# Where a planner may emit products of zeros, and where ScalarE's queue carries the first loads

## The chip, the cores and the metric

The kernel runs on one NeuronCore of a Trainium2 chip. The metric is the device time of one execution in microseconds (us); the median of three runs before is 318.51 us (318.28 to 318.63). The profile speaks of five engines: PE (matrix products; PEld is its weight load), DVE (vector), ACT (scalar), POOL (general) and SP (which here only issues transfers).

## The reference

A gated linear attention feeds a mixture of four attention experts. Cut to what is computed:

```python
# stage 1: q, k, v, alpha are (4, 8, 768, 48); state starts at 0
for t in range(S):
    state = alpha[:, :, t, :, None] * state + k[:, :, t] outer v[:, :, t]
    y[:, :, t] = q[:, :, t] @ state
x = y, heads side by side            # (4, 768, 384)
# stage 2: for each of 4 experts e, heads of 64
q, k, v = x @ wq[e], x @ wk[e], x @ wv[e]
a = softmax(causal(q @ k.T / 8))
ye = a @ v @ wo[e]
out += (e in the top 2 of x @ w_gate) * softmax_of_top2 * ye
```

## The kernel before

Stage 1 is cut into 24 chunks of 128 steps (6 for each of 4 batches); per chunk `n` the decays `alpha` become running products (two scans on DVE, `prep_r` and `prep_c`), are multiplied into queries and keys (`prep_kq`), and PE forms the chunk's inner products (`gla_a`, line 217), turns the keys (`gla_t`, line 234), updates the state (`gla_u`, line 263) and forms the output (`gla_y`, line 302). Three chunks make a unit; there are 8. Per unit stage 2 projects (lines 325 and 351), scores (400), takes exponentials on ACT (425), scales by the gate on POOL (437), turns the probabilities (452), multiplies with values (477) and with the output weights (496), and stores.

The order of all this is written by a planner in `run` (line 767). It holds, for each engine, the time at which it thinks the engine free (`free`), takes the candidate with the best value, emits it, and goes on. All engines run their emitted list in order and wait on semaphores. Eight PSUM banks `g0` to `g7` (matmul outputs) are handed out by the same planner.

Two places matter here. First, where the planner expects PE to sit idle for more than `IDLE` = 0.1929 us before the next operation, it fills the gap (lines 842 to 847): it takes the bank that comes free first, and `warm(i, k)` (line 884) emits products of a tile `d1r` with itself into that bank, `64 * k` columns wide, at most 512 a call. Nothing reads the result (the tile holds small constants; the title calls these products of zeros). Each call is one 32-bit product that PE runs as two passes, so the profile has two records a call. Line 847 then marks the bank as taken up to the planned start, with or without the products. Second, `opening` (line 892) writes the start by hand: SP issues the two halves of chunk 0's decays (`load_al(0, i, SY)`), ACT copies a one-element tile, ACT issues the two halves of chunk 0's queries and keys (`load_q(0, i, A)`), the constants are set up (mostly on POOL, among them the identity `ident`, line 157), and ACT copies the negated identity into `nid` (line 915), which waits for POOL. Then SP issues the loads of the next chunks and of the weights, and `warm(7, 32)` (line 939) emits four calls of 512 columns.

Transfers signal their landing on eight semaphores, DMAHW0 to DMAHW7, that are given out in turn; the ninth transfer takes the first one's semaphore again, and its issuer first waits until that earlier transfer has landed.

Of the kernel before, what the change touches and what calls it, by code (L numbers as in the profile page):

```python
# [12 lines left out]
AF = mybir.ActivationFunctionType  # L13
# [13 lines left out]
P = 112  # L27
# [9 lines left out]
    P="t.0 u.0 a.0 wx.v.0 a.1 t.1 wx.v.1 y.0 u.1",  # L37
    V="r.0.0 c.0.0 r.0.1 c.0.1 kq.0.0 kq.0.1 r.1.0 c.1.0 kq.1.0 r.2.0 m.1.1 m.1.0 S.1 c.2.0 kq.2.0 xl.0 sa.1 kt.2 xl.1 kr.2 m.2.1 m.2.0 r.3.0 c.3.0",
    A="kr.0 kt.0 wvh m.0.1 m.0.0 wl.v.0 kt.1 kr.1 B.1 wl.v.1 wqh.0 xh.0 xh.1 B.2 vo.0.0 wqh.1 xh.2 kt.3 vo.0.1 ph.0.0.0 ph.0.0.1 woh ck.0 vo.0.2 ck.2 kr.3 B.3",
# [8 lines left out]
CHANGE.update({(x, "y"): 0.12 for x in "tfas"})  # L48
CHANGE.update({(x, "t"): 0.15 for x in "asy"})
CHANGE.update({(x, "f"): 0.2 for x in "asy"})  # L50
IDLE = 0.1929
SHARE = 0
HEAD = 0.012
# [10 lines left out]
def tile_gla_moe(ctx: ExitStack, tc: tile.TileContext, qk_d, al_d, v_d, wqk_d, wv_d, wo_d, nat_d, vn_d, out_d):  # L64
    nc = tc.nc
    V, A, G, PE, SY = nc.vector, nc.scalar, nc.gpsimd, nc.tensor, nc.sync
# [62 lines left out]
    ident = fixed("ident", [128, 128])  # L129
# [17 lines left out]
    nid = fixed("nid", [128, 128], F32R)  # L147

    def constants():
        G.memset(d1r, TINY)  # L150
        G.memset(d1r[:, :, 0:1], 1.0)
        for t in d1c:
            V.memset(t, TINY)
        G.memset(mask, 1.0)
        G.affine_select(mask, mask, [[1, C]], OP.is_ge, 0.0, base=-(C - 1), channel_multiplier=1)
        G.memset(ident, 0.0)
        G.affine_select(ident, ident, [[1, 128]], OP.not_equal, 1.0, base=0, channel_multiplier=-1)
        for t in ST:
            G.memset(t, 0.0)
        for t in unit["kt"]:  # L160
            G.memset(t.rearrange("t p (s d) -> t p s d", s=2)[:, :, :, D:64], 0.0)
        G.memset(acc, 0.0)
        for t in SM:
            G.memset(t, 0.0)
        for t in [t for i, t in enumerate(unit["T"]) if i not in WHOLE]:
            for r in (32, 96):
                G.memset(t[r:r + 32, 3], 0.0)
        G.memset(cmask, 0.0)
        G.affine_select(cmask[:, 384:512], cmask[:, 384:512], [[-1, 128]], OP.is_ge, -1.0e30, base=0, channel_multiplier=1)
        G.memset(lm, 0.0)  # L170
        G.affine_select(lm, lm, [[1, NE], [-1, NE]], OP.is_gt, SMALL, base=0, channel_multiplier=0)
# [588 lines left out]
    for u in range(NU):  # L760
        k = len(ops)
# [5 lines left out]
    def run(start, arrive, busy):  # L767
        ENG = "PVAGS"
        free = dict.fromkeys(ENG, start)
# [35 lines left out]
        while todo:  # L805
            best = {}
            for o in cand:
                base = None
                need = {}
                for name in o["take"]:  # L810
                    pool = POOL.get(name[0], name[0])
                    need[pool] = need.get(pool, 0) + 1
                room = []
                for pool, k in need.items():
                    z = sorted((s[0], s[1]) for s in slots[pool] if s)
                    if len(z) < k:
                        room = None
                        break
                    room.append(z[k - 1])
                if room is None:  # L820
                    continue
                for alt in o["alts"]:
                    e = alt[0]
                    if first[e] and first[e][0] != o["key"] or e not in bound.get(o["key"], e):
                        continue
                    t = free[e]
                    for d in o["deps"]:
                        x, f = done[d]
                        t = max(t, x + hand(f, e) + (MARGIN if e == "P" else 0.0))
                    for x, f in room:  # L830
                        t = max(t, x + hand(f, e))
                    if e == "P":
                        t = max(t, free[e] + SWITCH * CHANGE.get((mode, o["mode"]), 0.0))
                    if e == "G" or o["lock"] and e == "V":
                        t = max([t] + [x[1] for x in lock["V" if e == "G" else "G"][-4:] if x[0] <= t])
                    v = t - free[e] + (PULL[e] if free[e] > 34.0 or e == "S" else HEAD) * (o["target"] - free[e])
                    if e not in best or v < best[e][0]:
                        best[e] = (v, t, o, alt)
            assert best, [o["key"] for o in cand][:30]
            e = min(best, key=lambda x: best[x][1])  # L840
            _, t, o, alt = best[e]
            if e == "P" and free["P"] > start and t - free["P"] > IDLE:
                x, i = min((s[0], i) for i, s in enumerate(slots["g"]) if s)
                k = int((t - max(x, free["P"]) - IDLE) / 0.11)
                if k > 0:
                    warm(i, k)
                    slots["g"][i] = [t, "P"]
            for name in o["take"]:
                pool = POOL.get(name[0], name[0])
                i = min((s[0], i) for i, s in enumerate(slots[pool]) if s)[1]  # L850
                slots[pool][i] = None
                where[name] = (pool, i)
            cand.remove(o)
            if first[e]:
                first[e].pop(0)
            alt[2]()
            dur = alt[1] * (SLOW if e in "VAG" else 1.0)
            end = t + dur
            free[e] = max(end - LAP[e], t + 0.04)
            if o["lock"] == 1 and e == "V":  # L860
                lock["V"].append((t, end))
            if e == "G":
                lock["G"].append((t, end))
            if e == "P":
                mode = o["mode"] or mode
            if o["land"]:
                busy = max(busy, t + 1.2) + KB.get(o["key"][0], 0.0) / RATE
                end = max(end + o["land"], busy)
            for name in o["uses"]:
                give(name, end, e)  # L870
            if len(alt) > 3:
                k = dict(key=o["key"], target=o["target"], deps=[("half", o["key"])], alts=[alt[3]], uses=[], take=[], mode="", land=0.0,
                         lock=False, n=0)
                done["half", o["key"]] = (end, e)
                cand.append(k)
                continue
            done[o["key"]] = (end, e)
            todo -= 1
            for w in waiting.get(o["key"], ()):
                w["n"] -= 1  # L880
                if not w["n"]:
                    cand.append(w)

    def warm(i, k):
        while k > 0:
            n = 64 * min(k, 8)
            PE.matmul(unit["g"][i][:, 0:n], zb[:, 0:128], zb[:, 0:n], start=True, stop=True)  # L887
            k -= 8
# [3 lines left out]
    def opening():  # L892
        arrive, z = {}, [LEAD]

        def came(key, kb):
            z[0] += kb / RATE
            arrive[key] = (z[0], "S")

        for n in range(4):
            where["T", n] = ("T", n)  # L900
        for n in range(3):
            where["v", n] = ("v", n)
        where["al", 0] = ("at", 0)
        plain = list(range(UNITS["al"]))
        for n in range(1, 4):
            where["al", n] = ("a", (2 * n - 2, 2 * n - 1)) if n in WHOLE else ("al", plain.pop(0))
        where["at", "wqk"], where["at", "wvo"] = ("at", 1), ("at", 2)
        for i in (0, 1):
            load_al(0, i, SY)
        G.memset(ones, 1.0)  # L910
        A.activation(ones, ones, AF.Copy)
        for i in (0, 1):
            load_q(0, i, A)
        constants()
        A.activation(nid, ident, AF.Copy, scale=-1.0)
        for key, kb in (("La", 0, 0), 264), (("La", 0, 1), 264), (("Lq", 0, 0), 262), (("Lq", 0, 1), 262):
            came(key, kb)
        z[0] += 0.3
        for n in (1, 2):
            load_al(n, 0, SY)  # L920
            load_q(n, 0, SY)
            load_v(n - 1)
            came(("La", n, 0), 132 * tiles(n))
            came(("Lq", n, 0), 131 * tiles(n))
            came(("Lv", n - 1), 262)
            if n == 1:
                SY.dma_start(wv, wv_d)
                came(("Lw", 1), 400)
        SY.dma_start(wqk, wqk_d)
        came(("Lw", 0), 786)  # L930
        load_v(2)
        came(("Lv", 2), 262)
        load_al(3, 0, SY)
        load_q(3, 0, SY)
        came(("La", 3, 0), 396)
        came(("Lq", 3, 0), 393)
        SY.dma_start(wo, wo_d)
        came(("Lw", 2), 393)
        warm(7, 32)
        return arrive, z[0]  # L940
# [159 lines left out]
```

## Time and profile before

| | |
|---|---|
| median of three runs | 318.51 us |
| the profiled execution | 318.76 us, of it 317.0 us from the first to the last instruction |
| granted TensorE clock, mean | 0.996 |
| line 887 (the products of line 887 in all) | 54 records, 27 calls |
| POOL busy | 128.2 us (40%) |
| ACT busy | 208.9 us (66%) |

Busy time is an average over the whole span; an engine that is busy all the time need not be doing work that the result needs. The chain of waits is the list of what ended last, followed back from the end: what stands on it sets the time, so long as nothing else is close behind. A window row gives the busy time of each engine in a stretch; the number in front of the engines is the stretch's length.

### The profile page before, as it was taken

The page shows a single profiled execution, that of the slowest core. Times are in us where ns is not written, and L with a number is a line of the kernel's source. Part 1 is how long each engine was busy: PE and PEld are TensorE (multiplying, and loading weights), DVE is VectorE, ACT ScalarE, POOL GpSimd, SP SyncE. Part 2 cuts the span into 40 slices and gives each one's busy share as a digit, 9 for nine tenths or more (in the row PEclk, how much of TensorE's full clock was granted, in tenths as well). Part 3 has the DMA queues.
Part 4 walks back from the last instruction along what each step waited for, and adds up shares of the span by engine and source line. Part 5 has one row for each costly group of instructions (what it writes and reads, how often), then busy time and mean ns, then how long its engine had stood idle before and what let it go on. Part 6 is the DMA issues. An engine that isn't in the chain of part 4 may idle for free.

```text
span 317.0 us, 11044 instructions
## 1 busy us (share of the span) xinstructions
PE 308.2 (97%) x4410; PEld 265.4 (84%) x4410; DVE 249.5 (79%) x678; ACT 208.9 (66%) x588; POOL 128.2 (40%) x197
## 2 busy tenths in 40 slices
PE   8999999999999999999999999999999999999992
PEld 3699989898997979889997988889897988888692
DVE  5999899998999998898998989675865754487620
ACT  2464986796785868578775776655964765377841
POOL 6334137516463483526343226414280344033510
PEclk9999999999999999999999999999999999999998
DMA  7996275543526246524354334304100000102001
GB/s 246 389 377 192 70 233 184 156 125 93 158 71 193 84 108 179 146 66 119 106 170 94 117 84 153 90 8 136 41 2 2 3 2 25 53 0 77 2 30 60
DMA packets 26893, 35.21 MB, mean 111 GB/s; under 512 B 2288, under 2 KB 22864, under 8 KB 26832
## 3 DMA queue, kind: packets, MB, share of 16 engines
q1 hardware_dynamic: 26144, 33.69, 34.6%
q8 instruction: 37, 0.61, 0.8%
q10 hardware_dynamic: 688, 0.72, 0.7%
q14 instruction: 24, 0.20, 0.2%
HBM read 27.61 MB, written 4.72 MB: 102 GB/s over the span
## 4 chain that ended last, share of the span: by engine, by line
PE 95%; DMA 1%; DVE 1%; ACT 0%; issue 0%; ACTq 0%; DVEq 0%
PE g L325 16%; PE g L452 13%; PE g L477 12%; PE g L302 11%; PE g L400 11%; PE g L351 8%; PE g L496 8%; PE g L217 7%; PE g L887 3%; PE g L263 2%; PE g L234 2%; DMA at<-in_al_dram 1%; DVE at L178 1%; PE g L721 0%; DVE T L198 0%
## 5 line engine op out<-in xcount | busy, mean ns | idle before, releaser
L437 POOL TENSOR_SCALAR a<-a,cf,gw 128x128 f32<-128x128 f32 (+5 forms) x96 | 80.5, 851 | 71.4 <-DVE cf L431 45.5
L425 ACT ACTIVATE a<-a,mx 128x256 f32<-128x256 f32 (+3 forms) x96 | 51.5, 539 | 9.1 <-DVE mx L414 9.0
L452 PE MATMUL g<-ident,a 128*128 128x128 f32 x336 | 53.7, 277 | 0.0
L325 PE MATMUL g<-x,wqkh 128*128 128x384 f32 x192 | 51.7, 350 | 0.0
L229 POOL TENSOR_SCALAR_AFFINE_SELECT ms<-ms 128x512 f32<-128x512 f32 x31 | 22.1, 724 | 56.2 <-ACT ms L225 56.2
L452 PEld LDWEIGHTS g<-ident,a 128*128 128x128 f32 x336 | 39.7, 140 | 5.8 <-issue 2.3
L240 DVE COPY at<-g 128x512 f32<-128x512 f32 (+3 forms) x62 | 29.2, 479 | 16.9 <-PE g L452 15.9
L477 PE MATMUL g<-at,vg 128*32 128x384 f32 (+2 forms) x648 | 39.7, 389 | 0.0
L400 PE MATMUL g<-k,q 64*128 64x256 f32 (+3 forms) x384 | 39.2, 336 | 0.0
L238 ACT ACTIVATE at<-g 128x512 f32<-128x512 f32 (+3 forms) x66 | 30.4, 465 | 8.4 <-PE g L452 6.6
L477 PEld LDWEIGHTS g<-at,vg 128*32 128x32 f32 x648 | 19.3, 109 | 18.5 <-issue 15.3
L302 PE MATMUL g<-ms,v 128*32 128x128 f32 x768 | 33.0, 274 | 0.0
L325 PEld LDWEIGHTS g<-x,wqkh 128*128 128x128 f32 x192 | 33.0, 189 | 0.0
L400 PEld LDWEIGHTS g<-k,q 64*128 64x128 f32 x384 | 28.6, 185 | 5.2 <-issue 2.3
L325 PE MATMUL g<-x,wqkl 128*128 128x384 f32 x96 | 32.3, 337 | 0.0
L351 PE MATMUL g<-wvh,x 128*128 128x260 f32 x144 | 31.7, 296 | 0.0
L414 DVE CUSTOM_DVE_ANT_0 a<-g,cmask 128x128 f32<-128x128 f32 (+2 forms) x64 | 28.2, 483 | 2.0 <-PE g L400 1.8
L496 PE MATMUL g<-woh,yy 128*128 128x384 f32 x96 | 28.1, 351 | 0.0
L217 PE MATMUL g<-T 48*128 48x128 f32 x384 | 25.7, 275 | 0.0
L217 PEld LDWEIGHTS g<-T 48*128 48x128 f32 x384 | 24.0, 187 | 1.3 <-DVE T L198 0.4
L351 PEld LDWEIGHTS g<-wvh,x 128*128 128x128 f32 x144 | 24.0, 190 | 0.4 <-ACT ms L225 0.4
L302 PE MATMUL g<-T,S 112*32 112x128 f32 x480 | 24.2, 272 | 0.0
(113 smaller groups left out, 616.1 us busy)
## 6 DMA issues: line engine op xcount, KB each, us to landing
al<-in_al_dram SPq DMA_DIRECT2D x21, 387.0 KB, 3.9
T<-in_qk_dram SPq DMA_DIRECT2D x21, 384.0 KB, 4.2
v<-in_v_dram SPq DMA_DIRECT2D x24, 256.0 KB, 4.5
out_dram<-ot SPq DMA_DIRECT2D x23, 192.0 KB, 2.1
T<-T SPq DMA_DIRECT2D x42, 48.2 KB, 2.2
a<-in_al_dram SPq DMA_DIRECT2D x2, 516.0 KB, 6.7
T<-in_qk_dram SPq DMA_DIRECT2D x2, 512.0 KB, 7.1
at<-in_wqk_dram SPq DMA_DIRECT2D x1, 768.0 KB, 8.5
```

The lines of the kernel that those rows point to most:

```text
L217: PE.matmul(pa[s][:, C * p:C * p + C], t[r:r + D, p, C:2 * C], t[r:r + D, p, 0:C], start=True, stop=True, tile_position=(r, 0))
L238: A.activation(out, src, AF.Copy)
L240: V.tensor_copy(out, src)
L302: PE.matmul(o[32 * j:32 * j + 32, k], l, r, start=(i == 0), stop=(i == len(parts) - 1), tile_position=(0, 32 * j))
L325: PE.matmul(pj[:, :W3], w[:, kt, cs], x[:, kt, :], start=(i == 0), stop=(i == 8))
L351: PE.matmul(pv[:, 0:260], x[:, kt, 128 * i:128 * i + 128], w[:, kt, :], start=(m == 0), stop=(m == 8))
L400: PE.matmul(sc(u, pair, i, e, x, c1 - c0), q[r, i0, ts], k[r, i1, c0:c1], start=(y == 0), stop=(y == 2), tile_position=(64 * e, 0))
L425: A.activation(a[:, c0:c1], src, AF.Exp, bias=mx[:, 1:2], scale=-1.0 if last else 1.0, accum_out=sm[:, x:x + 1])
L437: G.tensor_scalar(a[:, 0:n], a[:, 0:n], CF[u % 2][:, 3 * pair + i, e:e + 1], gw[:, u, i, eg:eg + 1], op0=OP.mult, op1=OP.mult)
L452: PE.transpose(pt[:, 128 * (j - j0):128 * (j - j0) + 128], a[:, 128 * j:128 * j + 128], ident)
L477: PE.matmul(o[r:r + 32, lo:n1], v[:, j % 3, 64 * eg + x:64 * eg + x + 32], at(("at", u, pair, e))[:, min(j, 4), at_off(j) + lo:at_off(j) + ...
L496: PE.matmul(po[:, 0:DM], y[:, h, 128 * i:128 * i + 128], w[:, pair, :], start=(m == 0), stop=(m == 5))
```

## The change

A constant `START` = 32.0 is added; the gap filler emits its products only where the planner's time for PE is below it. The mark on the bank is kept, so every later choice of the planner stays as it was. In the opening, the constants and the copy into `nid` are written before the two loads of chunk 0's queries and keys on ACT.

```diff
+START = 32.0
@@ run
                 k = int((t - max(x, free["P"]) - IDLE) / 0.11)
                 if k > 0:
-                    warm(i, k)
+                    if free["P"] < START:
+                        warm(i, k)
                     slots["g"][i] = [t, "P"]
@@ opening
         A.activation(ones, ones, AF.Copy)
+        constants()
+        A.activation(nid, ident, AF.Copy, scale=-1.0)
         for i in (0, 1):
             load_q(0, i, A)
-        constants()
-        A.activation(nid, ident, AF.Copy, scale=-1.0)
```

Of the 27 calls 16 go: their widths are 64, 192, 64 and 448 columns in PE's list up to its 45th us, then six of 64, and near the end 320, 128, 64, 128, 64 and 128. PE's list is otherwise the same, operation for operation and bank for bank. The fourth of them stands between two outputs of stage 1 (`ms`, `v`, `T`, `S` are masked products, values, queries with keys, and state). PE before:

```order
202 L302 MATMUL g_104<-ms_67,v_92 32x128 x8
203 L302 MATMUL g_104<-T_85,S_114 32x128 x4
204 L887 MATMUL g_105<-d1r 128x448
205 L302 MATMUL g_106<-ms_68,v_93 32x128 x4
206 L302 MATMUL g_106<-T_86,S_115 32x128 x4
```

And now, PE at the same place:

```order
199 L303 MATMUL g_104<-ms_67,v_92 32x128 x8
200 L303 MATMUL g_104<-T_85,S_114 32x128 x4
201 L303 MATMUL g_106<-ms_68,v_93 32x128 x4
202 L303 MATMUL g_106<-T_86,S_115 32x128 x4
203 L303 MATMUL g_106<-ms_68,v_93 32x128 x4
```

One call is gone and its neighbours have closed up; the second output still goes to the same bank.

The other place is the head of ACT's list, with the semaphores that each row waits for (`T_85` holds chunk 0's queries and keys). ACT before:

```order
2 L911 ACTIVATE ones<-ones 128x1 [waits Pool_49]
3 L122 DMA T_85<-in_qk_dram 128x2x256 x2
4 L915 ACTIVATE nid<-ident 128x128 [waits Pool_49]
5 L238 ACTIVATE kt_69<-g_101 128x3x2x16 [waits PE_49]
6 L238 ACTIVATE kt_69<-g_101 128x6x48
```

And now, ACT:

```order
2 L913 ACTIVATE ones<-ones 128x1 [waits Pool_49]
3 L915 ACTIVATE nid<-ident 128x128 [waits Pool_49]
4 L123 DMA T_85<-in_qk_dram 128x2x256 [waits DMAHW0_49]
5 L123 DMA T_85<-in_qk_dram 128x2x256 [waits DMAHW1_49]
6 L239 ACTIVATE kt_69<-g_101 128x3x2x16 [waits PE_49]
```

The two loads have moved behind the copy, and each has got a wait: they are now the ninth and tenth transfer in the order in which the semaphores are given out, and so wait for the landing of the first and the second, which are the two halves of chunk 0's decays on SP. In turn two SP loads, of chunk 2's decays and of its queries and keys, have lost theirs. SP before (`a` and `at_63` hold decays, `at_65` and `at_64` weights, `v` values):

```order
5 L927 DMA at_65<-in_wvg_dram 128x780
6 L118 DMA a<-in_al_dram 128x2x516 [waits DMAHW0_49]
7 L122 DMA T_87<-in_qk_dram 128x4x256 [waits DMAHW1_49]
8 L125 DMA v_93<-in_v_dram 128x512 [waits DMAHW2_49]
9 L929 DMA at_64<-in_wqk_dram 128x1536 [waits DMAHW3_49]
```

And now, SP:

```order
5 L929 DMA at_65<-in_wvg_dram 128x780
6 L119 DMA a<-in_al_dram 128x2x516
7 L123 DMA T_87<-in_qk_dram 128x4x256
8 L126 DMA v_93<-in_v_dram 128x512 [waits DMAHW2_49]
9 L931 DMA at_64<-in_wqk_dram 128x1536 [waits DMAHW3_49]
```

SP's order is the same; only what its sixth and seventh rows wait for has changed.

## Rows read from the trace of the kernel before

**Rows 1.** The page: busy time of two engines, and the chain by engine and line.

```profile
PE 308.2 (97%) x4410; PEld 265.4 (84%) x4410; DVE 249.5 (79%) x678; ACT 208.9 (66%) x588; POOL 128.2 (40%) x197
...
PE 95%; DMA 1%; DVE 1%; ACT 0%; issue 0%; ACTq 0%; DVEq 0%
```

**Rows 2.** PE's waits, whole span: total, times, longest (us).

```profile
PE g L234 <- issue: 0.6, 1, 0.6
PE g L234 <- ACT ms L225: 0.4, 1, 0.4
```

**Rows 3.** The chain of waits, 30 to 46 us: start, length, what.

```profile
32.27 0.36 PE g L887 x2
...
38.92 0.52 PE g L887 x2
...
41.76 0.36 PE g L887 x2
...
44.93 0.95 PE g L887 x2
```

**Rows 4.** Timeline of PE, 41 to 43 us: start, length, engine, line, tiles.

```profile
41.69 0.43 PE L887 MATMUL g<-d1r 128*128 128x64 f32 x2
41.93 0.37 PE L351 MATMUL g<-wvh,x 128*128 128x260 f32 x1
```

**Rows 5.** Windows: two stretches, then busy time of each engine in them.

```profile
32.00:64.00 32.00, 31.59 (x527) 27.95 (x514) 29.22 (x80) 25.48 (x74) 14.52 (x24) 1.00 0.53 159
76.00:290.00 214.00, 214.00 (x3001) 187.97 (x3003) 171.50 (x487) 145.76 (x419) 86.54 (x120) 1.00 0.29 84
```

**Rows 6.** DVE's waits, 30 to 64 us.

```profile
DVE cf L430 <- ACT a L425: 0.9, 2, 0.7
...
DVE kt L240 <- PE g L234: 0.4, 1, 0.4
DVE st L272 <- PE g L263: 0.3, 1, 0.3
```

**Rows 7.** The chain of waits, 145 to 148 us.

```profile
146.31 0.36 PE g L887 x2
```

**Rows 8.** The chain of waits, 288 to 311 us.

```profile
293.18 0.74 PE g L887 x2
...
300.38 0.22 PE g L887 x2
...
308.16 0.36 PE g L887 x2
```

**Rows 9.** Timeline, ACT and PE, 293 to 294 us.

```profile
293.01 0.86 ACT L238 ACTIVATE at<-g 128x512 f32<-128x512 f32 x2
...
293.76 0.83 PE L452 MATMUL g<-ident,a 128*128 128x128 f32 x6
```

**Rows 10.** Transfers issued up to 4 us: KB each, median us to landing.

```profile
at<-in_al_dram SPq DMA_DIRECT2D x2, 258.0 KB, 4.2
...
T<-in_qk_dram ACTq DMA_DIRECT2D x2, 256.0 KB, 3.4
...
v<-in_v_dram SPq DMA_DIRECT2D x1, 256.0 KB, 6.5
```

**Rows 11.** The chain of waits, 0 to 9.5 us.

```profile
0.81 3.84 DMA at<-in_al_dram
...
7.84 1.28 DVE T L198 x2
```

**Rows 12.** Timeline of PE from 10.4 us, and of SP up to 4 us.

```profile
3.52 0.66 SPq L125 DMA_DIRECT2D v<-in_v_dram  x1
...
10.50 0.29 PE L263 MATMUL g<-v,kt 128*32 128x48 f32 x8
```

**Rows 13.** Groups of PE by form, up to 6.8 us, then 9.2 to 10.25.

```profile
L887 PE MATMUL g<-d1r 128*128 128x512 f32 x6 | 5.5, 1088 | 1.6 <-POOL d1r L151 1.6
...
L887 PE MATMUL g<-d1r 128*128 128x512 f32 x2 | 1.0, 594 | 0.0
```

## The prediction

> **What bounds the kernel now.** I read the busy times and the chain first, then PE's waits, then the pieces of the chain that are products of zeros, then windows. PE is busy 97% of the span and holds 95% of the chain [rows 1]. After the opening it waits twice, 0.6 us before its first key transposes and 0.4 us for one mask copy on ACT [rows 2]. So PE's list, played back to back, sets the time, and the reader is to see that products of zeros stand in that list as on the chain: 0.36, 0.52, 0.36 and 0.95 us for the first four that go [rows 3], 0.36 us for each of the six of 64 columns in the middle [rows 7], and 0.74, three of about 0.2 (one shown, 0.22) and 0.36 us near the end [rows 8]. A sixteenth comes after the last output product, when only ACT's copy and the store are left, and counts nothing. The planner put them where it expected PE to idle; the trace shows no idle time around them. What the rows can't say by themselves is whether PE would have waited there without them, so each stretch needs its own look at the engines behind PE.
>
> **First part: the zeros that go.** Gross, by the chain, they are 2.19 + 6 x 0.36 + 1.7 = 6.05 us. I take that apart in three.
>
> *30 to 64 us, 2.19 us gross.* Here PE is not alone. From 32 to 64 us PE is busy 31.59 of 32 us, and VectorE 29.22 [rows 5]: it has 2.78 us to spare, and part of that it spends waiting for ACT. If PE comes earlier, VectorE can follow only by waiting less for PE. Of its waits in this stretch 0.4 + 0.3 = 0.7 us are for PE, and the longest is 0.9 us for ACT [rows 6]. So of 2.19 us I expect PE to keep about 0.6; the rest comes back as waits of PE, on VectorE's or ACT's results, by the wait on ACT at the end of the stretch at the latest. The bounds are 0 (VectorE and ACT set the pace here alone) and 2.19 (all kept).
>
> *64 to 290 us, six calls.* VectorE is busy 171.50 and ACT 145.76 of 214 us, PE all 214 [rows 5], and PE has no wait of note in that stretch [rows 2]. What is cut from PE here is kept. How much one call is worth has two readings: 0.36 us in the chain, or 0.24 us from its first start to the next product's start, 41.69 to 41.93 [rows 4], which I use for this form since all calls of 64 columns look alike. The next product's first pass is itself longer behind a call of zeros, and without the call some of that stays, since a change from narrow to full weights costs either way. I take the middle, 0.30 us, and so 6 x 0.30 = 1.8 us, bounds 1.4 and 2.2.
>
> *290 to 311 us, 1.7 us gross.* The widest call here (0.74 us) stands in front of a turn of probabilities at 293.76 us that needs a bank which ACT is emptying: its two copies run from 293.01 for 0.86 us [rows 9], so the first is done only about 0.15 us before PE starts. That call was a wait all along, worth 0.1 us. The other four, 0.22, twice about 0.2 and 0.36 us, stand between PE's own pieces; less the 0.05 us a call from above I take 0.8 us. Together 0.9 us, bounds 0.6 and 1.7.
>
> Sum of the first part: 0.6 + 1.8 + 0.9 = 3.3 us saved; bounds 2.0 and 6.05.
>
> **Second part: the first loads.** The names say that the loads move behind a copy that waits for POOL. The list says more: they now wait for the landing of the two halves of the decays. Before, all four loads were issued at once, the first at 0.81 us [rows 11], and took 4.2 us (decays) and 3.4 us (queries and keys) to land, by the median of two [rows 10]; the first half of the decays landed at 0.81 + 3.84 = 4.65 us and released VectorE [rows 11].
> - The gain: with nothing of ACT's beside it, the first half lands earlier. No row shows it alone. Nearest is the same load's 3.84 us at the one end and the 3.4 us of ACT's pair, first in line, at the other; I take a little less than the latter, 3.1 us, because it now has the engines to itself: it lands at 3.9 us and VectorE starts its scans 0.75 us sooner.
> - The cost: the first half of queries and keys is issued at about 3.95 us, the second at about 4.7 (the second half of the decays took 2 x (4.2 - 3.84) = 0.7 us more than the first, an estimate for its distance). By the 3.4 us of before the second lands at 8.1, by 4.2 at 8.9, by the 6.5 us that a load of values took from 3.52 us, behind a full queue [rows 10, 12], at 11.2. The two products that need them start at 7.84 us and half of 1.28 us later, at 8.48 [rows 11].
> So VectorE's second product starts between 0.4 us earlier and 2.7 us later than before. PE follows it: its last key transpose waits for that product, and the state update behind it at 10.50 us needs values that land at 3.52 + 6.5 = 10.0 us in any case [rows 12]; so the gain is at most 0.4 us. ACT has nothing to do between the two loads and its key copies, so its own wait delays no one else; SP loses two waits early, but its queue has work in front of it throughout. I take 3.8 us to land, halfway between the first two readings: the second load lands at 8.5 us and the term is 0, bounds 0.4 gained and 2.7 lost. What is lost here stays, since PE has only one more wait after the opening, of 0.4 us [rows 2].
>
> The Trainium skill, "DMA: Bandwidth & Descriptors", section "Queues, rings and completion order", says that each transfer engine goes round the queues that have work, a packet at a time, so that ACT's loads need not stand behind all that SP has issued; by that the term would be near 0 or a small gain. No row here shows two queues full at once long enough to bear it out.
>
> **The sum.** 318.76 us for the profiled execution (317.0 us span, 1.76 us around it), less 3.3, less 0: 315.46 us. That execution stands 0.25 us above the median of 318.51; against the median I forecast 315.2 us.
>
> **Rivals.**
> - *All zeros come back whole.* The engines behind PE follow, and 6.05 us go: 312.5 us. For it: PE's share of the chain, and no wait beside the zeros. Against: VectorE's 29.22 of 32 us and the bank at 293.76 us.
> - *The loads come late.* The second half of queries and keys lands behind the values and the weights that SP has queued, at 10.0 to 11.2 us: 1.5 to 2.7 us lost at the start, 316.7 to 317.9 us. For it: 6.5 us for the values. Against: that load stood behind four others on its own queue, and ACT's queue is empty.
> - *Nothing comes back.* Each call was a wait in disguise, as the planner thought, and PE now waits as long: 318.5 us, no change. For it: the planner placed them so. Against: six stand where VectorE and ACT have a fifth of their time or more to spare.
> - *Slower: the clock falls in the opening.* With the loads at 11.2 us PE has nothing between the end of its first block of zeros and its last key transposes, where its pause was 0.6 us [rows 2]. A pass of 512 columns took 1088 ns in the first 6.8 us, at 1.2 GHz, and 594 ns after, at 2.4 [rows 13]. If the level falls again in that pause, PE works at half pace for as long as it did at first, 5.5 us in those rows, and loses half of that, 2.75 us. With 2.7 us for the late loads: 318.5 - 3.3 + 2.7 + 2.75 = 320.7 us. It decides only if both happen; the pause alone leaves the forecast on the faster side. The Trainium skill, "TensorE: Matmul & The Clock Gate", section "HAM oscillation", has this as a rule: bursts with pauses bring the clock back down. The trace shows 0.6 us of pause without it.
>
> **How the numbers follow.** The forecast (314.0 to 316.2 us) 0.68, all whole 0.08, late loads 0.14, nothing 0.05, slower 0.05. About 0.2% (0.64 us) is what a measurement of this kernel can tell from no change. Late loads count as faster but for a tenth or so; that gives faster 0.88, same 0.06, slower 0.06. The range of 313.4 to 317.3 us leaves out the two ends of the rivals.
>
> **What would show it.** Right: no record of line 887 after 30 us; new short waits of PE between 38 and 64 us, on ACT or VectorE, of about 1.6 us in all; the stretch from 64 to 290 us shorter by 1.8 us; PE's turn at 293 us waiting for ACT. VectorE's first scan near 4.0 us instead of 4.74, and its second product near 8.5. Wrong: PE's waits in the middle grow by as much as the calls that went; the first product of queries after 9 us; a 128x512 pass near 1 us after the opening.

## The result: slower by 1.5%

The changed kernel takes 323.28 us, the median of six runs from 321.35 to 324.33; the kernel before took 318.40 beside it (six runs, 318.16 to 318.77). The ratio is 1.0145, 95% interval 1.0107 to 1.0183. Its runs are ordered by the mean granted clock: 324.0 to 324.3 us at 0.976 and 0.977, 321.4 and 321.9 at 0.988 and 0.989. The forecast was 315.2 us with a range up to 317.3: wrong in sign, and it came out as its own slower rival said, only further. The profiled execution took 324.0 us (span 322.2), 5.2 us more span than before.

The page of the changed kernel: busy time, the granted clock in 40 slices, and the chain by engine.

```profile
PE 309.1 (96%) x4378; PEld 264.8 (82%) x4378; DVE 250.0 (78%) x678; ACT 208.0 (65%) x588; POOL 127.9 (40%) x197
...
PEclk9659999999999999999999999999999999999999
...
PE 84%; DVE 5%; DMA 5%; ACT 4%; issue 0%; SPq 0%; ACTq 0%; DVEq 0%
```

Against [rows 1], 32 matmul records are gone (16 calls of two), yet PE is busier, 309.1 against 308.2 us, and its share of the chain fell from 95 to 84%. The reader is to see both reasons: some slices near the start have a clock of about half, and DMA and DVE now hold a tenth of the chain. The chain of the changed kernel, 0 to 22 us:

```profile
1.57 3.15 DMA at<-in_al_dram
...
4.75 8.97 DMA T<-in_qk_dram
...
13.82 0.70 DVE T L199
...
14.57 0.48 PE g L235
15.04 2.13 PE g L889 x4
17.18 0.79 PE g L264 x29
17.97 2.01 PE g L218 x16
```

Where [rows 11] had the decays and then VectorE, one transfer of queries and keys now stands for 9 us. The timeline of the changed kernel, 1.5 to 17 us, by engine; in brackets the idle time ahead and what ended it:

```profile
1.58 6.35 PE L889 MATMUL g<-d1r 128*128 128x512 f32 x8 [1.58 <-POOL d1r L152]
...
4.08 1.21 ACTq L123 DMA_DIRECT2D T<-in_qk_dram  x2
...
4.16 0.70 DVE L179 TENSOR_TENSOR_SCAN at<-at,d1r 128x258 f32<-128x258 f32 x1 [2.14 <-DMA at<-in_al_dram]
...
11.69 0.69 DVE L199 TENSOR_TENSOR T<-T,at 128x512 f32<-128x512 f32 x1 [4.34 <-DMA T<-in_qk_dram]
...
12.48 0.66 PE L235 MATMUL g<-ident,T 128*128 128x128 f32 x2 [4.54 <-DVE T L199]
...
13.82 0.69 DVE L199 TENSOR_TENSOR T<-T,at 128x512 f32<-128x512 f32 x1 [1.44 <-DMA T<-in_qk_dram]
...
14.57 0.48 PE L235 MATMUL g<-ident,T 128*128 128x128 f32 x1 [1.43 <-DVE T L199]
```

The first scan came early, as meant (4.16 us; 4.74 before). Its products with queries and keys waited for their loads until 11.69 and 13.82 us, where before they ran back to back from 7.84 [rows 11]. PE, out of zeros at 7.9 us, stood idle for 4.54 and 1.43 us. PE's waits of the changed kernel, whole span (total, times, longest):

```profile
PE g L235 <- DVE T L199: 6.0, 2, 4.5
...
PE g L453 <- ACT at L239: 0.6, 1, 0.6
PE g L453 <- POOL a L438: 0.2, 1, 0.2
PE g L235 <- ACT ms L226: 0.2, 1, 0.2
```

The two waits of [rows 2] have become five. Windows of the changed kernel (length, busy time of PE, PEld, DVE, ACT and POOL, then granted clock, DMA share, GB/s), and two of the kernel before:

```profile
10.00:14.00 4.00, 0.66 (x2) 0.29 (x2) 0.87 (x2) 0.00 (x0) 0.00 (x0) 0.55 1.07 371
14.00:24.00 10.00, 9.43 (x74) 6.75 (x74) 5.62 (x7) 2.87 (x6) 1.55 (x4) 0.50 1.05 384
24.00:64.00 40.00, 39.77 (x693) 35.89 (x692) 37.06 (x87) 27.93 (x77) 17.07 (x24) 1.00 0.46 144
```

```profile
10.00:14.00 4.00, 4.00 (x68) 2.95 (x68) 3.90 (x5) 2.52 (x5) 1.34 (x3) 1.00 1.08 384
14.00:24.00 10.00, 10.00 (x257) 8.52 (x253) 9.68 (x18) 5.46 (x12) 4.46 (x7) 1.00 1.05 381
```

From 14 to 24 us PE got through 74 products where it did 257, at half clock (1.2 GHz) and with little to do. By the trace's clock records it fell at 10.4 us, in the pause, and rose at 24.0.

PE's list is the same in both kernels but for the zeros, so the start of the same product in both traces gives a running difference: +9.8 us by 19 us, +8.9 at 64 us, +7.6 at 293, +6.9 at PE's last outputs, +5.2 at the end of the span. The opening costs 9.8 us and everything after it gives back 4.6.

### The profile page after: what moved, and what is told of

It is laid out like the page before. It is cut to its first block, busy times and chain, and to the rows that moved or that the text cites. A ratio compares the mean times of both kernels' runs of the same rounds, so it can differ in the third digit from the quotient of the medians.

```text
span 322.2 us, 10980 instructions
## 1 busy us (share of the span) xinstructions
PE 309.1 (96%) x4378; PEld 264.8 (82%) x4378; DVE 250.0 (78%) x678; ACT 208.0 (65%) x588; POOL 127.9 (40%) x197
## 4 chain that ended last, share of the span: by engine, by line
PE 84%; DVE 5%; DMA 5%; ACT 4%; issue 0%; SPq 0%; ACTq 0%; DVEq 0%
PE g L326 14%; PE g L453 12%; PE g L478 11%; PE g L303 9%; PE g L401 9%; PE g L497 8%; PE g L352 7%; PE g L218 6%; DMA T<-in_qk_dram 3%; PE g L235 2%; PE g L264 2%; ACT a L426 2%; DVE al L179 2%; DMA al<-in_al_dram 1%; PE g L889 1%; DMA at<-in_al_dram 1%
## 5 line engine op out<-in xcount | busy, mean ns | idle before, releaser
L230 POOL TENSOR_SCALAR_AFFINE_SELECT ms<-ms 128x512 f32<-128x512 f32 x31 | 21.2, 695 | 57.7 <-ACT ms L226 57.7
L218 PE MATMUL g<-T 48*128 48x128 f32 x384 | 28.0, 288 | 0.0
L218 PEld LDWEIGHTS g<-T 48*128 48x128 f32 x384 | 26.0, 199 | 2.0 <-issue 1.1
```

The costliest lines, as they stand in the source:

```text
L218: PE.matmul(pa[s][:, C * p:C * p + C], t[r:r + D, p, C:2 * C], t[r:r + D, p, 0:C], start=True, stop=True, tile_position=(r, 0))
```

## Experiments

In each, PE's start times are set against those of the kernel before in the same way. Unless a median of before is given, it was 318.36 us.

**Each part alone.** The zeros go, the opening stays as before:

```diff
+START = 32.0
-                    warm(i, k)
+                    if free["P"] < START:
+                        warm(i, k)
```

> The 16 calls go, the opening is as before. Theory A (the change lost all its time in the opening, and the zeros are worth what the changed kernel won back after it): PE reaches the key transposes of chunk 2 at 28.8 us instead of 18.9, 9.9 us late, but ends only 5.2 us late, so 4.7 us came back; at least the 3.3 us forecast for the zeros and at most 4.7 should show here: 313.7 to 315.1 us. Rival B (the zeros filled waits; what came back after the opening was idle time of the other engines catching up): 318.4 us, within 0.6.

314.52 us (314.40 to 315.43), ratio 0.9887, interval 0.9870 to 0.9905: 3.84 us faster. It has the lowest median of the study and is quicker than the kernel before and the changed one. Its two longest waits of PE after the first product:

```profile
PE g L235 <- issue: 1.2, 1, 1.2
PE g L453 <- ACT at L239: 0.6, 1, 0.6
```

The first is the pause ahead of the key transposes, the second the turn of probabilities that was [rows 9]; its timeline, ACT and PE:

```profile
291.23 0.86 ACT L239 ACTIVATE at<-g 128x512 f32<-128x512 f32 x2
...
291.95 0.74 PE L453 MATMUL g<-ident,a 128*128 128x128 f32 x5 [0.56 <-ACT at L239]
```

The turn now waits 0.56 us for ACT's copy, where a 0.74 us call of zeros stood. By stretch the difference moves by -0.7 us from 32 to 64 us, -1.4 to 290 us, -0.7 to 309 us, and by another -1.7 behind PE's last output, which no theory had; the opening was 0.3 us later.

The other part alone, with all zeros kept:

```diff
-START = 32.0
+START = 1000.0
```

> The loads move as in the change, all calls of zeros stay. Theory A: the 9.9 us lost by the 18.9th us stay, less what the zeros are not there to give: 318.4 + 9.9 - (0 to 3) = 325 to 328.3 us, with the granted clock at half for about 13.7 us. Rival B (zeros worth nothing): as the changed kernel, 323.3 us.

327.71 us (325.72 to 329.76), ratio 1.0301 (1.0244 to 1.0359): 9.35 us slower. Queries and keys landed at 11.1 and 13.1 us, the clock was at half from 9.7 to 23.4. The difference is +9.1 us by 16 us and stays. So the loads alone cost more than the whole change does, and the two parts add up: 9.35 - 3.84 = 5.5, against 4.9 measured.

**The clock held.** The changed kernel, with five more 512-column calls of zeros in the opening:

```diff
-        warm(7, 32)
+        warm(7, 72)
```

> The changed kernel with five more calls of 512 columns of zeros in the opening, which cover most of PE's pause from 8.0 to 12.5 us. Theory C (of the 9.9 us in the opening about half is the clock): the granted clock stays at 1.0 after 7 us, the loads are as late as in the change; PE works at full pace from 14.6 us, where it worked at half pace up to 24.0: 4.7 us less, about 318.6 us, and less spread from run to run. Rival D (the late loads alone cost it, the clock is hidden by waits on VectorE): 323 us as in the change.

320.56 us (320.06 to 321.37), ratio 1.0078 (1.0061 to 1.0096). Its timeline from 2.6 us:

```profile
2.60 9.61 PE L889 MATMUL g<-d1r 128*128 128x512 f32 x17
...
11.64 0.69 DVE L199 TENSOR_TENSOR T<-T,at 128x512 f32<-128x512 f32 x1 [4.34 <-DMA T<-in_qk_dram]
...
12.43 0.41 PE L235 MATMUL g<-ident,T 128*128 128x128 f32 x2 [0.23 <-DVE T L199]
...
13.65 0.69 DVE L199 TENSOR_TENSOR T<-T,at 128x512 f32<-128x512 f32 x1 [1.32 <-DMA T<-in_qk_dram]
...
14.40 0.33 PE L235 MATMUL g<-ident,T 128*128 128x128 f32 x1 [1.55 <-DVE T L199]
```

and its windows, to be held against those of the changed kernel:

```profile
10.00:14.00 4.00, 2.61 (x8) 0.86 (x6) 1.04 (x2) 0.00 (x0) 0.00 (x0) 1.00 1.07 378
14.00:24.00 10.00, 9.60 (x201) 7.42 (x201) 9.73 (x12) 5.87 (x13) 2.71 (x5) 1.00 1.05 385
```

The loads are as late as in the changed kernel, the clock stays at 1.00, and 201 products fit into the stretch that had 74. So of the changed kernel's time the clock is 323.28 - 320.56 = 2.7 us by medians (3.9 by the two profiled executions), less than the 4.7 that theory C asked for, and the late loads are the rest of the loss: at 16 us PE is 5.2 us behind the kernel before.

**Why the loads land so late.** The changed kernel, with one more one-element set on POOL that makes SP's sixth load wait, so that ACT's two get semaphores of their own and wait for no landing:

```diff
         G.affine_select(ident, ident, [[1, 128]], OP.not_equal, 1.0, base=0, channel_multiplier=-1)
+        G.memset(raw[2][:, 0:1], 0.0)
```

> The changed kernel, with one column of the weights' tile set to zero by POOL right after the identity, so that SP's sixth load waits for POOL and the two loads on ACT get the seventh and eighth semaphore: they stand behind the copy but wait for no landing, and are issued at about 2.6 and 3.1 us. Theory E (the wait for the landing made them late): they land 3.4 to 4.2 us after issue, by 7.3 us, VectorE's second product is not late, the clock stays, and the time is that of the zeros alone, 313.7 to 315.1 us. Rival F (they are late since SP's transfers issued before them are served first): issued 1.5 us sooner, they land only some 2 us sooner than in the change, the second at 11 to 12 us, and the time is 319 to 322 us.

318.39 us, ten runs from 316.18 to 320.94, ratio 0.9990 (0.9962 to 1.0018). Its timeline:

```profile
2.58 1.02 ACTq L123 DMA_DIRECT2D T<-in_qk_dram  x2
...
9.01 0.69 DVE L200 TENSOR_TENSOR T<-T,at 128x512 f32<-128x512 f32 x1 [1.76 <-DMA T<-in_qk_dram]
...
9.80 0.41 PE L236 MATMUL g<-ident,T 128*128 128x128 f32 x2 [1.88 <-DVE T L200]
...
10.58 0.69 DVE L200 TENSOR_TENSOR T<-T,at 128x512 f32<-128x512 f32 x1 [0.88 <-DMA T<-in_qk_dram]
...
11.33 0.47 PE L236 MATMUL g<-ident,T 128*128 128x128 f32 x1 [1.12 <-DVE T L200]
```

Issued 1.5 us sooner, the loads' products start 2.7 and 3.2 us sooner. The wait for the decays' landing thus costs about 3 us of the 5.35 that the second product is late. Theory E fails, since the loads still took 6.4 and 7.4 us to land and not 3.4 to 4.2; F holds in the main, though the second landed at 10.5 us, before the 11 to 12 that it gave, and the median lies 0.6 us under its range. The clock still fell in the profiled execution, from 10.4 to 20.6 us, in the stretch with the pauses of 1.88 and 1.12 us. It did not do so every time, and the runs are ordered by it: at a mean granted clock of 0.997 they took 316.2 and 316.5 us, at 0.992 to 0.994 from 318.0 to 318.7, at 0.982 from 320.4 on.

Then the same with SP held at its third load in place of its sixth, so that only the decays are issued before ACT's first load:

```diff
+        G.memset(early[1][0][:, 0:1], 0.0)
```

> The changed kernel, with one column of chunk 1's decays set to zero by POOL right after the identity: SP's third load waits for POOL, so ACT's two loads, still behind the copy, are issued at about 2.6 us with nothing but the two halves of the decays ahead of them, and wait for no landing. Theory F (served in the order of issue): they land by 6 and 7.5 us, VectorE's second product is at 7.7 to 8 us, the clock stays, and the time is that of the zeros alone or a little less, 314.2 to 314.8 us. Rival (a load on ACT's queue beside a busy SP queue is slow however it is placed): the second lands after 9 us, as with no wait, and the time is 316 us or more.

315.50 us (315.16 to 318.24), ratio 0.9905 (0.9888 to 0.9921), before 318.93. The profiled execution was the slowest of five, the only one with a mean clock below 0.997; it has half clock from 10.5 to 13.9 us. There the products start at 8.34 and 10.06 us:

```profile
2.59 0.94 ACTq L123 DMA_DIRECT2D T<-in_qk_dram  x2
...
2.62 0.54 SPq L119 DMA_DIRECT2D a<-in_al_dram  x1
...
3.20 0.61 SPq L123 DMA_DIRECT2D T<-in_qk_dram  x1
...
9.14 0.41 PE L236 MATMUL g<-ident,T 128*128 128x128 f32 x2 [1.13 <-DVE T L200]
...
10.80 0.47 PE L236 MATMUL g<-ident,T 128*128 128x128 f32 x1 [1.26 <-DVE T L200]
```

That is only 0.5 to 0.7 us sooner than with SP's third and fourth load ahead: what is issued beside the loads costs them nearly as much as what is issued ahead. The landings, at 8.3 and 10.0 us, are as the rival said (the second after 9) and not by 6 and 7.5, but the time lies between the two forecasts.

Last, queries and keys on SP's own queue, right behind the decays:

```diff
+        for i in (0, 1):
+            load_q(0, i, SY)
         ...
-        for i in (0, 1):
-            load_q(0, i, A)
```

> The zeros go; the two loads of chunk 0's queries and keys are issued by SP, right behind the decays and ahead of all else, and ACT issues none. Theory F (transfers are served in the order in which they were issued): decays land at 4.06 us as in the changed kernel, 0.6 us sooner than before, queries and keys by 6.3, VectorE starts 0.6 us sooner, and the time is 0.1 to 0.4 us under the zeros alone: 314.1 to 314.4 us. Rival: with one queue the engines' transfers are slower than with two, VectorE's second product comes after 8.5 us, and the time is 314.6 to 315.5 us.

319.41 us, ratio 0.9967 (0.9924 to 1.0009), before 318.93. The runs fall into two groups: four from 315.2 to 316.0 us at a mean clock of 0.997 or more, the others from 319.4 us on at 0.988 or less. The products start at 7.28 us, 0.56 sooner than before, but the loads behind them on SP are later (the values land at 11.7 us, 10.0 before), and PE has to wait for these, as its waits show:

```profile
PE g L264 <- DMA v<-in_v_dram: 1.8, 1, 1.8
...
PE g L235 <- DVE T L199: 1.1, 1, 1.1
```

In the profiled execution the clock was at half from 11.8 to 18.6 us. So this order lands queries and keys sooner than the other moves do, and gives the time back at the values and, in some runs, by the clock: the two groups lie some 3.8 us apart. Neither forecast holds: the median is later than both, and the second product comes at 7.9 us, before the rival's 8.5.

**The clock once more.** The kernel of 318.39 us with two more calls of zeros, which fill the 1.88 us pause:

```diff
-        warm(7, 32)
+        warm(7, 48)
```

> Kernel: the changed kernel with its first query and key loads behind the copies but without the wait for the decays' landing (issued at 2.6 us), as in the run of 316.2 to 320.9 us, and with four more 512-column products of zeros in the opening, so that PE's pause of 1.9 us before its first key transposes is filled. Theory C (the spread and the median of that run are the clock's fall): granted clock full from 7 us on, times within about 1 us, near 316.3 us, its lowest. Theory D (the loads' own landing varies): spread and median stay, 316 to 321 us, clock full.

317.70 us, ten runs from 316.50 to 319.66, ratio 0.9972 (0.9951 to 0.9993), before 318.80. The profiled execution has the clock full from 6.5 us on, and PE waits only once in the opening after that, 1.14 us. No run fell to the 0.982 of the kernel without the fill, and the slowest, at 0.987, is 1 us quicker than its slowest. But the median moved by only 0.7 us, and one run took 318.25 us at 1.000: the clock is a part of the spread there, how large a part is open, and neither theory holds whole.

**The zeros below 32 us.** The version with the opening of before and no later zeros, with the seven calls that the change keeps removed as well:

```diff
-START = 32.0
+START = 0.0
```

> The zeros alone, and the seven calls below 32 us go too (640 columns before the first state update, then four of 64 and one of 192), so that only the opening's block is left. If the opening is set by PE, about 0.2 to 0.5 us less than with the zeros alone, 314.0 to 314.3 us (the values that the first update needs land at 10.0 us, so the 1.25 us of the first two give 0.4 at most). Rival: the calls hold the clock where PE waits, the granted clock falls to half near 10.4 us as in the changed kernel, and the time is 317 to 319 us.

316.56 us (315.54 to 317.53), ratio 0.9932 (0.9908 to 0.9957), before 318.93. This is faster than before and 1.4 us (by the ratios) to 2.0 us (by the medians) slower than with these seven calls. Neither forecast holds. In the opening of the profiled execution PE pauses for 1.8 and 0.6 us before and after its first key transposes, at full level, and for 1.1 us more at 20.5 us; from 22.3 to 25.7 us the clock was at half. By the start times this execution loses 1.4 us at that last pause and as much again at half clock, of which 0.5 us comes back by 32 us. So the early zeros are worth their time.

**The last 1.7 us.** At the end all engines meet twice. In the kernel before, the others leave the first meeting at 314.8 us and PE at 316.65; in the version without zeros all leave it at 312.3. First, the fast version with its opening block of zeros cut into 20 calls, so that PE's list is as long as before's:

```diff
-        warm(7, 32)
+        for n in 8 * [2] + 12 * [1]:
+            warm(7, n)
```

> The zeros alone, as before, but the opening's block of zeros is cut into 20 calls (8 of 128 and 12 of 64 columns) in place of four of 512, so that PE's list is again as long as in the kernel before (20 calls for 4 gives back the 16 that went). In the kernel before, and where only the loads move, PE's last barrier release comes 1.6 to 1.9 us after the other engines' and right behind a 16 KB fetch of instructions; with the 16 calls gone it comes within 0.02 us of theirs. Theory G (that lag hangs on the length of PE's list, and is part of what the zeros gave): the lag is back and the time is 1.5 us over the zeros alone, about 316.0 us. Rival H (the lag belongs to the last call of zeros itself): no lag, 314.5 us.

318.33 us, ten runs, ratio 1.000 (0.9973 to 1.0027), before 318.93. Nearly all of the gain is gone: in the profiled execution 1.2 us on the way (0.9 of it near 24 us, 0.5 near 224), and the rest at the end, which takes 7.6 us from the start of PE's last product, where the fast version needs 5.0 and before 6.4. So it is later than both theories had it. Then only the sixteenth call kept, and only the sixteenth removed:

```diff
+                    if free["P"] < START or free["P"] > 330.0:
```

> Kernel: before, without fifteen of the sixteen later calls of zeros; the sixteenth, two products of 128 columns behind the last output product, is kept. The version without all sixteen took 314.5 us and was 1.7 us better at the very end than PE's own list explains: in before, PE left the program's end 1.9 us behind the other engines, there at the same time. Theory L (the sixteenth call itself does that): the 1.7 us are lost again, about 316.2 us, with PE last at the end. Theory F (the end is late by where PE's list ends, its length; this kernel's is four records longer than the fast one, twenty-eight shorter than before's): no loss, about 314.5 to 314.8 us, all engines at the end together.

315.18 us (314.68 to 315.59), ratio 0.9884 (0.9865 to 0.9902), before 318.80. No lag: all engines leave the first meeting at 313.3.

```diff
+                    if free["P"] < 330.0:
```

> Kernel: before, without the sixteenth call of zeros alone; the other fifteen are kept. Theory L (the call behind the last output product delays the end): 318.4 - 1.7 = 316.7 us, all engines at the end together. Theory F (length or place of the list): the list is four records shorter than before's, so the lag of PE at the end stays, about 318.4 us.

316.97 us (316.76 to 317.55), ratio 0.9951 (0.9932 to 0.9970): 1.83 us gained by one call that nothing waits for, 1.7 of it behind PE's last output by the traces. All engines leave the first meeting at 314.3.

Each of the two theories failed in one of these runs: the sixteenth call does not cause the lag where the other fifteen are gone, and its removal alone cures it. What orders the traces is the number of PE's matmul records: before has 4410 [rows 1], and the kernel without the sixteenth call, by its page:

```profile
PE 307.8 (98%) x4406; PEld 264.6 (84%) x4406; DVE 249.0 (79%) x678; ACT 208.9 (66%) x588; POOL 128.7 (41%) x197
```

The three kernels with 4410 (before, the loads alone, the cut block) take 6.1 to 7.6 us from the start of PE's last product to the end; the others, with 4406 or fewer, 4.8 to 5.1. So it goes with where PE's list ends, not with what stands last in it. Code pieces of 16 KB are still being fetched in these last microseconds, in the quick kernels too; in the kernel before, the last of them is over at 315.4 us, 1.2 us before PE goes on. That PE waits for code was not shown, and the cause stays open.

## Why the prediction was wrong

*What bounds the kernel, and the zeros: right in the main.* 3.3 us were forecast, 3.84 measured with this part alone. The terms: 0.6 forecast for 30 to 64 us, 0.7 measured in this trace, but that is partly luck: 0.17 of it is a shorter wait for ACT at 63.7 us, which is shorter by about 0.35 in the two kernels that remove nothing there (the loads alone, and the sixteenth call alone), and in five later kernels the stretch gives less than 0.1 (below); 1.8 for the six calls in the middle, 1.4 measured, so the 0.24 us of [rows 4] was a better reading than the middle that I took; 0.9 for the tail, 0.7 measured, with PE's turn at ACT's copy as foretold. That is 2.8 instead of 3.3. What brings the sum back up is 1.7 us behind PE's last output, for which I had no term: I said of the sixteenth call that it "counts nothing", and its removal alone gave 1.83 us, though with the other fifteen gone it may stay at little loss (3.62 us gained against 3.84). In the changed kernel the same pieces are worth 0.8, 1.3, 0.7 and 1.8 us.

The first of these terms has a reading that I missed. Of the five traces with the later zeros gone (all, or all but the sixteenth) that give less than 0.1 us there, each has the same wait, here in the one that keeps only the sixteenth call:

```profile
45.24 0.69 PE L303 MATMUL g<-T,S 112*32 112x128 f32 x5 [0.82 <-ACT S L281]
```

The product that reads the state `S` waits 0.82 us for ACT's copy of it, close behind the place where the call of 448 columns (0.95 us in [rows 3]) stood. So in these traces that call was nearly all a wait, while the other five traces keep 0.7 to 0.95 us of the stretch. What decides between the two stays open. I also read [rows 6] wrongly: 0.9 us is the sum of two waits for ACT, and the longest is 0.7.

*The first loads: the step that failed.* The term was 0, with 2.7 us as its worst bound. The gain came as forecast: the first half of the decays landed at 4.06 us (3.9 forecast), and the two loads were issued at 4.1 and 4.7. The landing was mis-sized: I took 3.8 us, halfway between two readings of the program's start, and they took 7.6 and 9.0, more than the 6.5 that I held as the worst. VectorE's second product came at 13.82 us, not 8.5, 5.35 us later than before. The reason stood in [rows 10, 12], where I read the values' 6.5 us as the price of standing behind four loads "on its own queue" and called ACT's queue empty. The DMA views of the changed kernel, 4.1 to 8.2 and 8.4 to 12.8 us, by queue (q1 SP, q10 ACT: packets, MB, share of the engines' time):

```profile
q1 hardware_dynamic: 829, 1.11, 95.0%
```

```profile
q1 hardware_dynamic: 616, 1.19, 72.1%
q10 hardware_dynamic: 524, 0.51, 33.9%
```

For the first 4.2 us after its issue ACT's load moves no packet at all, while SP's loads keep the engines 95% busy. The delay from issue to the first packet grows with what SP has issued before: 1.1 us at the start of the kernel before, 1.6 and 2.0 with SP held at its third and sixth load, 4.2 here. Then the two queues take nearly equal numbers of packets, and ACT's, of about 1 KB to SP's 2, have 30% of the bytes. The round that the Trainium skill describes in "DMA: Bandwidth & Descriptors", "Queues, rings and completion order", shows from 8.3 us on; I read from it a term near 0, and the 4.2 us before the first packet are against that reading. What holds the first packet back was not isolated.

*The slower rival: right in mechanism, wrong in size and chance.* It asked for late loads and a fall of the clock and got 0.05. The two aren't independent: with zeros until 7.9 us and products at 11.2 the pause follows from the lateness. Priced at 2.7 + 2.75, they cost 5.35 and, by the kernel with the clock held, 2.7 us by medians and 3.9 in the profiled executions. The stretch at half level, taken as 5.5 us from the first such stretch, was 13.7. "HAM oscillation" of the Trainium skill's page "TensorE: Matmul & The Clock Gate" is the rule that bore out here (half level from 10.4 us, in a pause of 4.54 us), where [rows 2] had only a 0.6 us pause to weigh it by. With the measured terms the sum is 318.76 + 9.8 - 0.8 - 1.3 - 0.7 - 1.8 = 324.0 us, the profiled execution; it closes by construction, since the terms are differences of start times in the two traces.

*What would show it.* Most signs were the right ones: a first product after 9 us was named as the mark of failure. No zeros after 30 us of before's time, the wait on ACT at the turn, and the first scan near 4.0 us came as written. The new waits of about 1.6 us between 38 and 64 us did not: with the zeros alone one of 0.23 us for POOL is on record there, in the five traces above 0.82 for ACT besides, and the middle became shorter by 1.4 us, not 1.8. A pass of 512 columns near 1 us came back too: the four behind the key transposes took 2.34 us instead of 1.25 in all, at half level.

## What to carry to other kernels

A load that moves behind others is priced by what all queues have in flight at its new issue time, not by its own queue, and a load that reuses a semaphore also inherits an earlier landing. Where a late input leaves PE with nothing to do, the clock's fall belongs in the same case as the lateness, at full price. The two halves of a change are best judged apart: here one is worth 3.8 us and the other costs 9.4.

## What the runs showed of the hardware

- PE's pauses in the opening, and the clock after them: 0.61 us (before), 1.17 (zeros alone), 0.23 and 1.55 (clock held) kept full level; 1.13 and 1.26 (SP held earlier), 1.88 and 1.12 (no landing wait), 1.10 and 1.8 (SP's queue), and 4.54 and 1.43 (the change) lost it in the profiled executions. With the early zeros gone, 1.76 and 0.64 us kept it, and the fall at 22.3 us came behind a pause of 1.11 us. So the length of the pauses alone does not sort these cases, and one and the same kernel (SP held earlier, SP's queue) keeps its level in some runs and loses it in others, for 3 to 4 us.
- The end of the program took 6.1 to 7.6 us from the start of PE's last product in the three kernels with 4410 matmul records, 4.8 to 5.1 in the others; one call of zeros less was worth 1.83 us. Why was not shown.
- Two 256 KB loads took 7.6 and 9.0 us to land behind SP's backlog, 6.4 and 7.4 when issued 1.5 us earlier, 3.4 by the median at the very start [rows 10].
